# Two w_o groups of a decode kernel are loaded in two parts, one of them through a source with an outer dimension of 8

## The chip, the cores and the metric

The kernel runs on one core of a Trainium2 chip. The metric is the device time of one execution in microseconds (us); lower is better. A core has a matrix engine (PE, with its weight loads shown apart as PEld), a vector engine (DVE), a scalar engine (ACT), GpSimd (POOL), and SyncE (SP), which here does nothing but issue loads. Loads and stores are carried by 16 DMA engines that all issuers share.

## What is computed

One decode step: layer norm of a row x of 576 values, then two branches on it that are added to x. Branch A is attention with one query: 32 query heads, 16 key/value heads of 128, over the last 4096 positions of the caches, and a product with `wo`. Branch B is a gated MLP with sequence length 1. All tensors are bfloat16.

```python
xn = _layernorm(x, axis=-1)
# A
q = (xn @ wq).reshape(B, Sq, Hq, Dh).transpose(0, 2, 1, 3)
k = jnp.repeat(k_cache[:, :, Sk - W:, :], 2, axis=1)
v = jnp.repeat(v_cache[:, :, Sk - W:, :], 2, axis=1)
p = _softmax(jnp.einsum('bhqd,bhkd->bhqk', q, k) * Dh ** (-0.5), axis=-1)
o = jnp.einsum('bhqk,bhkd->bhqd', p, v)
a = o.transpose(0, 2, 1, 3).reshape(B, Sq, Hq * Dh) @ wo      # wo is 4096 x 576
# B
z = _gelu(xn @ w_in)                                          # w_in is 576 x 4608
g = w_sp * _layernorm(z[..., Fh:], axis=-1) + b_sp
b = (z[..., :Fh] * g) @ w_out                                 # w_out is 2304 x 576
out = x + a + b
```

Some 51 MB have to be read for a result of 576 values: 16 K and 16 V blocks of 1 MB, wq 4.7 MB, w_in 5.3 MB, wo 4.7 MB, w_out 2.7 MB.

## The kernel before, in words

**Loads.** All large loads are issued by SP, in program order, before any arithmetic of the program text: `load_kv` (line 81), `load_rows` (line 95, for wq, w_in and w_out) and `load_wo` (line 101). Their order is: K of heads 0 and 1, wq in five parts, and then for b = 1 to 8 the K of block b (two heads), the V of block b - 1, and a piece of w_in (b = 1 to 3) or one w_o group (`load_wo(b - 4)` for b = 4 to 6; in block 8 `load_wo(3)` stands in the place of K); at the end w_out in four parts of 8, 6, 3 and 1 rows a partition. Each load goes to a tile of the pool `units`, which has 18 buffers, and has one of eight completion semaphores in turn: a load is issued when the load eight before it, with the same semaphore, has landed. x and the two scalars of branch B come through ACT's queue (lines 70, 343, 344).

**A w_o group.** wo has 4096 rows; group j is rows 1024 j to 1024 j + 1023. `wo_v` gives partition p the eight consecutive rows 1024 j + 8 p + r, r = 0 to 7, as one run of 8 x 576 values, 9216 B. One load of 128 such runs fills the tile (line 101).

**Attention.** For each block b of two key/value heads, `T` (lines 203 to 207) transposes eight 128 x 128 pieces of K on PE and copies them out of PSUM on DVE or ACT, `S` (line 215) makes the scores, `sm_max`, `sm_tr`, `sm_exp` and `sm_rec` do the softmax, `PV` (line 258) multiplies with V, and `O` (line 263) writes four columns of `oTn`, 128 x 32, one column a query head: the head's 128 output values over the partitions.

**The product with wo.** In `oTn` the row 1024 j + i of wo belongs to partition i mod 128 of column 8 j + i div 128, while the tile has it at partition i div 8 and row r = i mod 8. `O_perm(j)` moves the values over: for each r a matmul (line 268) with `selr[:, r]`, which picks the partitions congruent to r modulo 8 and repeats them over the eight columns, gives all eight columns in every partition; line 271 multiplies with the mask `hm`, which keeps the one column that belongs to the partition (partitions 16 n to 16 n + 15 keep column n); line 273 adds up. The result, `oP[:, j, r]`, is the weight of the matmuls of `WO(j)` (line 277, through `out_mm`): 8 rows r in four column groups of 144, 32 matmuls a group. `selr` is made on DVE (line 189), `hm` too (line 133).

**Order.** The loop over b (lines 360 to 390) is the order of PE. `O_perm(j)` stands in blocks 2, 4, 6 and 8, `WO(j)` in blocks 4, 5, 6 and 8 (`wo_at`). The 18 rows of w_out follow as 72 matmuls of line 277, then line 395 copies the sum out of PSUM and line 396 stores it.

Of the kernel before, what the change touches and what calls it, by code (L numbers as in the profile page):

```python
# [8 lines left out]
FP32 = mybir.dt.float32  # L9
BF16 = mybir.dt.bfloat16  # L10
ALU = mybir.AluOpType
# [3 lines left out]
P = 128  # L15
D = 576
# [16 lines left out]
FR = FH // P  # L33
UNITS = 18
KTB = 12


@with_exitstack
def kernel(
# [14 lines left out]
    nc = tc.nc  # L54
    ctx.enter_context(tc.manual_schedule())

    const = ctx.enter_context(tc.tile_pool(name="const", bufs=1))
    work = ctx.enter_context(tc.tile_pool(name="work", bufs=2))
    units = ctx.enter_context(tc.tile_pool(name="units", bufs=UNITS))
    ktp = ctx.enter_context(tc.tile_pool(name="ktp", bufs=KTB))  # L60
    PS = bass.MemoryType.PSUM
# [11 lines left out]
    kn, vn, wq_t, win_t, wo_t, wout_t = {}, {}, {}, {}, {}, {}  # L73
    wq_v = A_wq.rearrange("k (s c) -> (k s) c", s=2).rearrange("(p r) c -> p r c", r=NS)
    win_v = B_w_in.rearrange("k (s c) -> (k s) c", s=2).rearrange("(p r) c -> p r c", r=NS)
    wo_v = A_wo.rearrange("(j p r) n -> j p (r n)", p=P, r=8)
    wout_v = B_w_out.rearrange("(p r) n -> p r n", r=FR)

    def load_kv(store, cache, name, h):
# [12 lines left out]
    def load_rows(store, view, name, width, cuts):  # L92
        for a, e in zip(cuts, cuts[1:]):
            t = units.tile([P, e - a, width], BF16, name=f"{name}{a}", tag="u")
            nc.sync.dma_start(t[:], view[:, a:e, :])
            for i in range(a, e):
                store[i] = t[:, i - a, :]

    def load_wo(j):
        t = units.tile([P, 8 * D], BF16, name=f"wo{j}", tag="u")  # L100
        nc.sync.dma_start(t[:], wo_v[j])
        wo_t[j] = t

    win_parts = {1: (0, 2, 4), 2: (4, 6, 8), 3: (8, 9)}
# [2 lines left out]
    for b in range(1, NB + 1):  # L107
        if b < NB:
            load_k(b)
        else:  # L110
            load_wo(NWO - 1)
        load_v(b - 1)
        if b in win_parts:
            load_rows(win_t, win_v, "win", FH, win_parts[b])
        elif b < 7:
            load_wo(b - 4)
# [3 lines left out]
    ident = const.tile([P, P], BF16, name="ident")  # L120
# [7 lines left out]
    ident_f = const.tile([P, P], FP32, name="ident_f")  # L128
# [3 lines left out]
    hm = const.tile([P, 8], FP32, name="hm")  # L132
    nc.vector.tensor_reduce(out=hm[:], in_=ident_f[:].rearrange("p (n q) -> p n q", n=8), axis=AXX, op=ALU.add)
    selr = const.tile([P, 8, 8, 16], BF16, name="selr")
    out_ps = ps_c.tile([P, OW], FP32, name="out_ps")
    nc.vector.memset(out_ps[:], 0.0)

# [49 lines left out]
        return xe_r[:, 2 * r:2 * r + 2]  # L187

    nc.vector.tensor_copy(selr[:], ident[:].rearrange("p (q r) -> p r q", r=8).unsqueeze(2).to_broadcast([P, 8, 8, 16]))


    kT, s_ps, p_sb, sm = {}, {}, {}, {}
    q_bf = const.tile([P, HQ], BF16, name="q_bf")
    oTn = const.tile([P, HQ], BF16, name="oTn")
    oP = const.tile([P, NWO, 8], BF16, name="oP")
# [68 lines left out]

    def O_perm(j):
        op = ps_m.tile([P, 8, 8], FP32, name=f"op{j}", tag="m")
        for r in range(8):
            nc.tensor.matmul(op[:, r, :], lhsT=selr[:, r, :, :].rearrange("p n q -> p (n q)"),  # L268
                             rhs=oTn[:, 8 * j:8 * j + 8], start=True, stop=True)
        tmp = work.tile([P, 8, 8], FP32, name=f"om{j}", tag="om")  # L270
        nc.vector.tensor_tensor(out=tmp[:], in0=op[:], in1=hm[:].unsqueeze(1).to_broadcast([P, 8, 8]), op=ALU.mult)
        with nc.allow_low_precision(reason="one of the eight is not zero, and it is a bfloat16 value"):
            nc.vector.tensor_reduce(out=oP[:, j, :], in_=tmp[:], axis=AXX, op=ALU.add)  # L273

    def out_mm(lhsT, rhs, start=False, last=False):
        for g in range(NCG):
            nc.tensor.matmul(out_ps[32 * g:32 * g + 1, :], lhsT=lhsT, rhs=rhs[:, OW * g:OW * (g + 1)],  # L277
                             start=start, stop=last, tile_position=(0, 32 * g))

    def WO(j):  # L280
        for r in range(8):
            out_mm(oP[:, j, r:r + 1], wo_t[j][:, D * r:D * (r + 1)])


    hv = const.tile([P, FR], BF16, name="hv")
# [50 lines left out]
    for r in range(NS):  # L336
        for c in range(16):
            nc.tensor.matmul(q_ps[:, c, :], lhsT=wq_t[r][:, P * c:P * (c + 1)], rhs=xe_of(r),  # L338
                             start=(r == 0 and c == 0), stop=r == NS - 1, skip_group_check=True)
# [5 lines left out]
    for g in range(NCG):  # L345
        nc.tensor.matmul(out_ps[32 * g:32 * g + 1, :], lhsT=one_bf[:, 0:1], rhs=x_row[:, OW * g:OW * (g + 1)],
                         start=True, stop=False, tile_position=(0, 32 * g))
# [12 lines left out]
    for b in range(1, NB + 1):  # L360
# [26 lines left out]
        if b % 2 == 0:  # L387
            O_perm(b // 2 - 1)
        if b in wo_at:
            WO(wo_at[b])  # L390
# [36 lines left out]
```

## Time and profile before

| | |
|---|---|
| median of 3 runs | 132.22 us (132.12 to 132.78) |
| profiled execution, its own time | 131.92 us |
| its span, first to last instruction | 130.1 us |
| PE, PEld busy | 106.3 us (82%), 100.7 us (77%) |
| DVE, ACT busy | 51.9 us (40%), 29.2 us (22%) |
| mean granted PE clock | 0.712 |
| bytes read | 50.96 MB, 392 GB/s over the span |
| chain of waits: DMA, PE, DVE | 45%, 44%, 6% of the span |
| a w_o load | 1152 KB, 20.6 us from issue to landing |

The profile is of one execution. Busy time is the time in which an engine ran an instruction; a matmul's end is modelled. "DMA share" is the mean busy share of the 16 DMA engines. "Landing" of a load is the moment when its semaphore has its full count. The chain of waits follows the execution back from its last instruction, at each step to what released it. Besides the summed rows the trace has a record of each DMA packet (queue, start, duration, bytes, but not which of the 16 engines ran it) and of each increment of a semaphore by a DMA.

### The profile page before, as it was taken

The page shows a single profiled execution, that of the slowest core. Times are in us where ns is not written, and L with a number is a line of the kernel's source. Part 1 is how long each engine was busy: PE and PEld are TensorE (multiplying, and loading weights), DVE is VectorE, ACT ScalarE, POOL GpSimd, SP SyncE. Part 2 cuts the span into 40 slices and gives each one's busy share as a digit, 9 for nine tenths or more (in the row PEclk, how much of TensorE's full clock was granted, in tenths as well). Part 3 has the DMA queues.
Part 4 walks back from the last instruction along what each step waited for, and adds up shares of the span by engine and source line. Part 5 has one row for each costly group of instructions (what it writes and reads, how often), then busy time and mean ns, then how long its engine had stood idle before and what let it go on. Part 6 is the DMA issues. An engine that isn't in the chain of part 4 may idle for free.

```text
span 130.1 us, 4613 instructions
## 1 busy us (share of the span) xinstructions
PE 106.3 (82%) x2133; PEld 100.7 (77%) x2133; DVE 51.9 (40%) x157; ACT 29.2 (22%) x38; POOL 0.7 (1%) x6
## 2 busy tenths in 40 slices
PE   3589518699899998989978798799899949994790
PEld 3489418499898997989977797699779939993780
DVE  4486000355402552054436624455444552454200
ACT  3136000033200360013604060233214401340000
POOL 2000000000000000000000000000000000000000
PEclk9999655556855599555995555557977985699559
DMA  4999999999999999999999999999999999999940
GB/s 116 420 431 431 420 412 422 418 420 429 411 415 420 421 416 419 413 415 418 423 415 418 424 425 408 430 411 420 418 422 412 420 421 416 415 420 417 388 158 0
DMA packets 7232, 51.24 MB, mean 394 GB/s; under 512 B 813, under 2 KB 942, under 8 KB 1454
## 3 DMA queue, kind: packets, MB, share of 16 engines
q1 hardware_dynamic: 7208, 50.96, 94.7%
q8 instruction: 16, 0.26, 0.8%
q14 instruction: 2, 0.02, 0.0%
q10 hardware_dynamic: 6, 0.00, 0.0%
HBM read 50.96 MB, written 0.00 MB: 392 GB/s over the span
## 4 chain that ended last, share of the span: by engine, by line
DMA 45%; PE 44%; DVE 6%; issue 1%; ACT 1%; ACTq 0%; SPq 0%
DMA k<-in_A_k_cache_dram 19%; PE tp L203 18%; DMA wout<-in_B_w_out_dram 14%; DMA wq<-in_A_wq_dram 12%; PE zp L294 8%; PE s L215 6%; PE o L258 5%; PE bc L234 2%; PE out_ps L277 1%; DVE m L227 1%; PE su L249 1%; PE tr L225 1%; PE op L268 1%; DVE mb L236 1%; ACT p L241 0%
## 5 line engine op out<-in xcount | busy, mean ns | idle before, releaser
L203 PE MATMUL tp<-ident,k 128*128 128x128 bf16 x512 | 53.0, 275 | 1.3 <-DMA k<-in_A_k_cache_dram 0.8
L203 PEld LDWEIGHTS <-k 128*128 128x128 bf16 x512 | 43.9, 128 | 2.7 <-issue 1.6
L207 DVE COPY kT<-tp 128x1024 bf16<-128x1024 bf16 x40 | 27.5, 690 | 23.5 <-PE tp L203 23.5
L205 ACT COPY kT<-tp 128x1024 bf16<-128x1024 bf16 x24 | 24.3, 1011 | 34.4 <-PE tp L203 34.4
L215 PE MATMUL s<-q_bf,kT 128*128 128x2 bf16 x512 | 21.0, 166 | 1.5 <-DVE kT L207 1.4
L215 PEld LDWEIGHTS <-kT 128*128 128x128 bf16 x512 | 19.9, 103 | 1.9 <-DVE kT L207 1.6
L258 PE MATMUL o<-p,v 128*128 128x2 bf16 x512 | 15.3, 164 | 0.1
L258 PEld LDWEIGHTS <-v 128*128 128x128 bf16 x512 | 14.4, 98 | 0.2 <-issue 0.2
L241 ACT ACTIVATE p<-d 128x128 bf16<-128x128 f32 x8 | 2.5, 310 | 49.9 <-DVE d L239 49.9
L294 PEld LDWEIGHTS <-win 128*128 128x128 bf16 x162 | 10.5, 162 | 1.6 <-issue 1.6
L294 PE MATMUL zp<-xe,win 128*128 128x2 bf16 x162 | 10.4, 200 | 1.1 <-DVE m L227 1.1
L338 PE MATMUL q_ps<-xe,wq 128*128 128x2 bf16 x144 | 4.5, 165 | 4.6 <-DMA wq<-in_A_wq_dram 4.6
L338 PEld LDWEIGHTS <-wq 128*128 128x128 bf16 x144 | 4.1, 101 | 4.9 <-DMA wq<-in_A_wq_dram 4.8
L234 PEld LDWEIGHTS bc<-dg,ones_f 4*128 4x128 f32 x16 | 3.2, 244 | 5.5 <-DVE dg L229 4.3
L234 PE MATMUL bc<-dg,ones_f 4*128 4x4 f32 x16 | 3.9, 309 | 4.0 <-DVE dg L229 3.1
L277 PE MATMUL out_ps<-wo,oP 128*1 128x144 bf16 x128 | 4.3, 296 | 1.8 <-DVE oP L273 1.6
L249 PEld LDWEIGHTS su<-ss,ones_f 128*128 128x128 f32 x16 | 4.3, 328 | 1.5 <-DVE ss L244 1.5
L249 PE MATMUL su<-ss,ones_f 128*128 128x4 f32 x16 | 4.4, 343 | 1.3 <-DVE ss L244 1.3
L220 DVE TENSOR_REDUCE mx<-s 128x4 f32<-128x128 f32 x8 | 2.3, 292 | 6.8 <-PE s L215 6.8
L277 PEld LDWEIGHTS <-oP 128*1 128x1 bf16 x128 | 2.9, 106 | 2.2 <-DVE oP L273 1.8
L244 DVE TENSOR_REDUCE ss<-p 128x4 f32<-128x128 bf16 x8 | 2.3, 286 | 3.2 <-ACT p L241 3.2
L340 DVE CAST q_bf<-q_ps 128x32 bf16<-128x32 f32 x1 | 0.3, 301 | 8.2 <-PE q_ps L338 8.2
(78 smaller groups left out, 41.3 us busy)
## 6 DMA issues: line engine op xcount, KB each, us to landing
k<-in_A_k_cache_dram SPq DMA_DIRECT2D x16, 1024.0 KB, 19.4
v<-in_A_v_cache_dram SPq DMA_DIRECT2D x16, 1024.0 KB, 20.6
win<-in_B_w_in_dram SPq DMA_DIRECT2D x4, 1152.0 KB, 18.9
wo<-in_A_wo_dram SPq DMA_DIRECT2D x4, 1152.0 KB, 20.6
wq<-in_A_wq_dram SPq DMA_DIRECT2D x4, 1024.0 KB, 10.9
wout<-in_B_w_out_dram SPq DMA_DIRECT2D x1, 1152.0 KB, 20.4
wout<-in_B_w_out_dram SPq DMA_DIRECT2D x1, 864.0 KB, 19.6
win<-in_B_w_in_dram SPq DMA_DIRECT2D x1, 576.0 KB, 19.3
```

Source lines behind the costliest of these rows:

```text
L203: nc.tensor.transpose(tp[:, i, :], kn[h][:, 8 * c + i, :], ident[:])
L205: nc.scalar.copy(kT[n][:], tp[:])
L207: nc.vector.tensor_copy(kT[n][:], tp[:])
L215: nc.tensor.matmul(s_ps[b][:, i, 8 * c + t, :], lhsT=kT[n][:, t, :], rhs=q_bf[:, 2 * h:2 * h + 2], start=True, stop=True)
L220: nc.vector.tensor_reduce(out=mx[:], in_=s_ps[b][:].rearrange("p i t r -> p i r t"), axis=AXX, op=ALU.max)
L234: nc.tensor.matmul(bc[:], lhsT=ones_f[0:4, :], rhs=sm[b]["dg"][:], start=True, stop=True)
L241: nc.scalar.activation(p[:], d[:], ACT.Exp, scale=SCALE)
L249: nc.tensor.matmul(su[:], lhsT=ones_f[:], rhs=sm[b]["ss"][:].rearrange("p i r -> p (i r)"), start=True, stop=True)
L258: nc.tensor.matmul(sm[b]["o"][:, 2 * i:2 * i + 2], lhsT=vn[2 * b + i][:, t, :], rhs=p_sb[b][:, i, t, :], start=t == 0, stop=t == NT - 1)
L277: nc.tensor.matmul(out_ps[32 * g:32 * g + 1, :], lhsT=lhsT, rhs=rhs[:, OW * g:OW * (g + 1)], start=start, stop=last, tile_position=(0, 32 ...
L294: nc.tensor.matmul(zp[:, c, :], lhsT=w_r[:, c, :], rhs=xe_of(r), start=(r == rows.start and c == 0), stop=r == rows.stop - 1, skip_group_c ...
L338: nc.tensor.matmul(q_ps[:, c, :], lhsT=wq_t[r][:, P * c:P * (c + 1)], rhs=xe_of(r), start=(r == 0 and c == 0), stop=r == NS - 1, skip_grou ...
```

## The change

Groups 0 and 3 are each loaded by two loads in place of one. The first brings rows r = 0 to n - 1 of each partition (n = 3 for group 0, 2 for group 3), 128 runs of n x 1152 B. Its source is written with the group's 1024 rows split as (q, a, r) = (16, 8, 8) and `a` taken outermost, so it has the dimensions 8 x 16 x (n x 576), and partition 16 a + q gets rows 64 q + 8 a + r, where before partition p had rows 8 p + r. The second load brings the rows from n on as before, 128 runs of (8 - n) x 1152 B. Groups 1 and 2 keep one load.

As these n rows stand at other partitions, `O_perm` needs another selection (`selw`) and another mask (`hmw`) for them; the multiplication with the mask is done in two pieces in groups 0 and 3. `hmw` is one more reduction on DVE at the start and `selw` three more copies of 128 columns, after `selr`. The matmuls keep their number and shapes.

```diff
+WIDE = {0: 3, 3: 2}
+NWIDE = 3
...
-    wo_v = A_wo.rearrange("(j p r) n -> j p (r n)", p=P, r=8)
+    wo_v = A_wo.rearrange("(j p r) n -> j p r n", p=P, r=8)
...
     def load_wo(j):
-        t = units.tile([P, 8 * D], BF16, name=f"wo{j}", tag="u")
-        nc.sync.dma_start(t[:], wo_v[j])
+        t = units.tile([P, 8, D], BF16, name=f"wo{j}", tag="u")
+        n = WIDE.get(j, 0)
+        if n:
+            nc.sync.dma_start(t[:, 0:n, :].rearrange("p r n -> p (r n)"),
+                              A_wo[1024 * j:1024 * (j + 1), :].rearrange("(q a r) n -> a q (r n)", a=8, r=8)[:, :, 0:n * D])
+        nc.sync.dma_start(t[:, n:8, :], wo_v[j][:, n:8, :])
         wo_t[j] = t
...
+    hmw = const.tile([P, 8], FP32, name="hmw")
+    nc.vector.tensor_reduce(out=hmw[:], in_=ident_f[:].rearrange("p (a n q) -> p n a q", a=8, n=8),
+                            axis=mybir.AxisListType.XY, op=ALU.add)
+    selw = const.tile([P, NWIDE, P], BF16, name="selw")
...
+    for r in range(NWIDE):
+        nc.vector.tensor_copy(selw[:, r, :].rearrange("p (a n q) -> p a n q", a=8, n=8),
+                              ident[:].rearrange("p (q a r) -> p r a q", q=2, a=8)[:, r].unsqueeze(2).to_broadcast([P, 8, 8, 2]))
...
     def O_perm(j):
         op = ps_m.tile([P, 8, 8], FP32, name=f"op{j}", tag="m")
+        n = WIDE.get(j, 0)
         for r in range(8):
-            nc.tensor.matmul(op[:, r, :], lhsT=selr[:, r, :, :].rearrange("p n q -> p (n q)"),
-                             rhs=oTn[:, 8 * j:8 * j + 8], start=True, stop=True)
+            sel = selw[:, r, :] if r < n else selr[:, r, :, :].rearrange("p n q -> p (n q)")
+            nc.tensor.matmul(op[:, r, :], lhsT=sel, rhs=oTn[:, 8 * j:8 * j + 8], start=True, stop=True)
         tmp = work.tile([P, 8, 8], FP32, name=f"om{j}", tag="om")
-        nc.vector.tensor_tensor(out=tmp[:], in0=op[:], in1=hm[:].unsqueeze(1).to_broadcast([P, 8, 8]), op=ALU.mult)
+        for a, e, mask in ((0, n, hmw), (n, 8, hm)):
+            if e > a:
+                nc.vector.tensor_tensor(out=tmp[:, a:e, :], in0=op[:, a:e, :],
+                                        in1=mask[:].unsqueeze(1).to_broadcast([P, e - a, 8]), op=ALU.mult)
...
     def WO(j):
         for r in range(8):
-            out_mm(oP[:, j, r:r + 1], wo_t[j][:, D * r:D * (r + 1)])
+            out_mm(oP[:, j, r:r + 1], wo_t[j][:, r, :])
```

## The prediction

> **What bounds the kernel now.** I read the DMA rows of the page first, then the last microseconds as a table of stretches, then the waits and the tail of the timeline, and last the trace's own records of DMA packets and semaphore landings.
>
> ```profile
> DMA  4999999999999999999999999999999999999940
> GB/s 116 420 431 431 420 412 422 418 420 429 411 415 420 421 416 419 413 415 418 423 415 418 424 425 408 430 411 420 418 422 412 420 421 416 415 420 417 388 158 0
> ...
> q1 hardware_dynamic: 7208, 50.96, 94.7%
> q8 instruction: 16, 0.26, 0.8%
> q14 instruction: 2, 0.02, 0.0%
> ```
>
> All 16 DMA engines are busy from slice 2 to slice 38. The q8 row is instructions, not data: 16 packets of 16 KB; 0.8% of 16 engines x 130.1 us is 16.7 us, so 1.04 us each, on one engine. The next rows (stretch, length, busy PE, PEld, DVE, ACT, POOL, then PE clock, DMA share, GB/s) show that the 16 engines do not finish together:
>
> ```profile
> 122.00:123.00 1.00, 0.60 (x18) 0.45 (x14) 0.28 (x2) 0.00 (x0) 0.00 (x0) 0.50 1.00 407
> 123.00:123.50 0.50, 0.08 (x7) 0.08 (x9) 0.33 (x2) 0.00 (x0) 0.00 (x0) 0.50 0.82 327
> 123.50:124.00 0.50, 0.50 (x24) 0.50 (x26) 0.00 (x0) 0.00 (x0) 0.00 (x0) 0.50 0.63 253
> 124.00:125.00 1.00, 1.00 (x44) 1.00 (x36) 0.00 (x0) 0.00 (x0) 0.00 (x0) 0.50 0.53 204
> 125.00:126.00 1.00, 1.00 (x40) 0.80 (x32) 0.00 (x0) 0.00 (x0) 0.00 (x0) 0.50 0.43 174
> 126.00:126.50 0.50, 0.38 (x16) 0.18 (x5) 0.00 (x0) 0.00 (x0) 0.00 (x0) 0.50 0.26 92
> ```
>
> About half of them are done by 124, the rest at 126.4. Shares times lengths from 123 on add up to 1.82 us, so perfectly shared work would end at 124.8: at most 1.6 us lie in balance. The landings say who is late. Every 128-row load raises its semaphore 16 times, once an engine; for the last wout part these come 0.00 to 0.32 us (six engines), 0.96 and 1.01, 1.71, and 3.10 to 3.34 us (seven) after the first, at 123.52. The same lags can be followed back load by load: each 16 KB packet of q8 puts one engine back by 1.55 us, always one of the same eight in turn; each 8 KB packet of q14 puts one of two others back by about 0.7.
>
> But PE ends at almost the same time:
>
> ```profile
> 122.89 0.23 DVE L271 TENSOR_TENSOR om<-op,hm 128x64 f32<-128x64 f32 x1 [0.44 <-PE op L268]
> 123.14 0.22 DVE L273 TENSOR_REDUCE oP<-om 128x8 bf16<-128x64 f32 x1
> ...
> 123.42 1.13 PE L277 MATMUL out_ps<-wo,oP 128*1 128x144 bf16 x32 [0.57 <-DVE oP L273]
> ...
> 124.33 2.05 PE L277 MATMUL out_ps<-wout,hv 128*1 128x144 bf16 x56
> ...
> 126.55 0.59 PE L277 MATMUL out_ps<-wout,hv 128*1 128x144 bf16 x16 [0.17 <-DMA wout<-in_B_w_out_dram]
> ```
>
> In the list of waits PE's only wait on a load after the first 21 us is this one:
>
> ```profile
> PE out_ps L277 <- DMA wout<-in_B_w_out_dram: 0.2, 1, 0.2
> ```
>
> PE ends its 56 matmuls at 126.38 and needs 0.59 for the last 16. Earlier loads alone can save 0.17 us; later loads cost nearly all that they are late.
>
> **The change, step by step.** *Who carries the moved rows.* The landings also show how a load is spread: one row (x_row) raises its semaphore once from a transfer, the output's four rows four times, 128 rows 16 times. A load with an outer dimension of 8 on one side should thus run on eight engines. [...]
>
> *Engine time.* From one packet's start to the next on its engine the records have 47 ns for 1152 B, 132 for 3456, 176 for 4608, 262 for 6912, 309 for 8192, 346 for 9216; between neighbours, 2304 B is 90 and 5760 B 219 (estimates). A w_o load is now 8 x 346 + 6 (semaphore) = 2774 ns on each engine. With three rows moved, all engines do 8 x 219 + 6 = 1758, and the eight carriers 16 x 132 + 6 = 2118 more: 3876, so +1102 for carriers and -1016 for the others. With two rows: 8 x 262 + 6 = 2102, carriers 16 x 90 + 6 more = 3548: +774 and -672. Together carriers +1.88, others -1.69 us.
>
> *Are the carriers the early ones?* The two 2-byte loads of lines 343 and 344 run on one engine, which is a carrier too if a load on fewer engines always takes the first ones. Their packets, at 15.13 and 16.06, push back the packets of one engine alone by 6 ns each. Following it, it becomes one of a pair that I can't part at 23.5; one of the pair takes the instruction packet of 24.5. The small loads' semaphores come 463 and 464 ns after their packet; the engine hit at 24.5 shows 448 on average, the other of the pair about 462. So I take the carriers for the early engines, at 4 to 1.
>
> *Full speed or not.* Eight carriers reach all 128 partitions, of which 16 engines have eight each in a plain load, so half of the wide packets or more go where another engine writes, beside its normal stream. No row shows two engines on each other's partitions. Lower bound: full speed, 0 extra. Upper bound: two engines share and each has half, so the wide 16 x 132 + 16 x 90 = 3.55 us take 3.55 more. Nearest row: the instruction packet, the only big one that does not go to its engine's own rows: 1.04 us where 16 KB at 309 ns per 8 KB would take 0.62, a factor of 1.7. I take 1.75, that is 0.75 x 3.55 = 2.66 us extra.
>
> [...]
>
> *Sum for the loads.* Carriers: 0.32 (the last without an instruction packet) + 1.88 + 2.66 = 4.86 us behind the first engine of now; those two with an 8 KB packet 1.01 + 1.88 + 2.66 = 5.55. Now the last is at 3.34. A landing waits for all engines, so the end moves by 5.55 - 3.34 = +2.2.
>
> *The rest.* Two more load issues on SP at 0.33 us: SP stands waiting for a landing eight loads back nearly all the time, and with some 20 us from issue to landing, two half loads among eight leave over 15 us of queued data; uncovered they would cost 0.66. That the second part waits for the first, both being of one tile, is unlikely: the two loads into ws2 were issued at 11.68 and 11.93, the first landed at 15.90. hmw: one reduce as hm's (0.28), in DVE's 0.86 us idle before line 147. Three selw copies: selr took 1.08 for 1024 columns, 128 each are some 0.2 (line 140's copy of 128): 0.6 us ahead of the first kT copy, covered by 8.2 us in which DVE waits for q_ps; uncovered 0.9 in all. O_perm of groups 0 and 3 has one more small multiply, about 0.2 us. For group 3 it lies between 122.89 and 123.42 on the way to WO(3), so PE's own tail would end 0.2 later, 0.03 after today's end; beside loads 2.2 late it is hidden. Matmuls and weight loads keep number and shape.
>
> Profiled execution 131.92 + 2.1 (PE was 0.1 us behind the last part) = 134.0; the median, 132.22, lies 0.30 above that execution: **134.3 us**, slower by 1.6%.
>
> **Rivals.** *Balance works, PE ends it.* Carriers early and at full speed: the ends are 0.32 + 1.88 = 2.20 and, with an 8 KB packet, 2.89 for carriers, 3.34 - 1.69 = 1.65 for the others: loads end 0.45 earlier, but PE's tail plus 0.2 gives +0.03: 132.25. For it: the moved time, 3.57 us between halves, fits the gap of 3.3. Against: full speed on foreign partitions is unproven. Chance 0.17. *Balance works and PE follows.* k and v land 1.0 us earlier from group 0 on; if PE or its clock (0.50 at the end) gained from it, the gain is 0.45 to 1.1 (the two 8 KB packets on other engines): 131.4. Against: PE's one 0.17 us wait. Chance 0.13. *Carriers are the late ones, or mixed.* Full speed: 3.34 + 1.88, the end +1.9: 134.1. Decided by the identity above. Chance 0.15. *The load does not narrow* and runs on 16: two semaphores and some more packets, 0.1 us: 132.3. Chance 0.05. *Forecast*, slowed carriers, 0.50; by its bounds from 132.2 (no extra) over 135.2 (half) up to some 137, where three writers meet (a third of the speed: 3.55 x 2 instead of 2.66, +4.4).
>
> **From these.** Its own range is 132.9 to 136.8; with the rivals 131.8 to 136.8. 0.5%, 0.66 us, is about what a measurement can tell from no change. Faster: 0.12. Within: 0.17 + 0.05 + 0.04 (low end of the forecast and of the gain) = 0.26. Slower: 0.62.
>
> **What would show it.** Landings of the two wide loads raised by eight engines; their packets of 3456 and 2304 B at more than 132 and 90 ns; the DMA share below 1 after about 124 for longer, with the end at 128 or later and PE waiting at line 277 for a wout part by 2 us. I am wrong if the wide packets keep 132 and 90 ns (then one of the full-speed rivals holds, and the order of the last landings says which), if 16 engines carry them, or if PE waits for k or v.

## The result and the profile after

| | before | after |
|---|---|---|
| median | 132.12 us (132.09 to 132.78, 6 runs) | 137.67 us (137.49 to 138.00, 6 runs) |
| ratio, 95% interval | | 1.0415 (1.0391 to 1.0438) |
| profiled execution; its span | 131.92; 130.1 us | 137.75; 136.0 us |
| last w_out load: landings of its 16 engines | 123.52 to 126.86 us | 125.92 to 132.76 us |

The change costs 5.55 us, 4.2%. The direction was foretold, the time lies 3.4 us above the forecast and 0.9 us outside the range. The page of the kernel after, its rows for DMA:

```profile
DMA  4999999999999999999999999999999999999710
GB/s 121 424 427 429 422 412 424 417 426 419 421 412 423 422 418 417 417 420 414 422 409 251 306 417 425 415 419 419 424 416 423 412 422 306 313 415 410 317 50 0
...
q1 hardware_dynamic: 7480, 50.96, 93.8%
q8 instruction: 16, 0.26, 0.8%
```

The bytes are those of before, and the engines are as busy as before, but in slices 21 and 22, and again in 33 and 34 (counted from 0, 3.4 us each), they move 251 to 313 GB/s where the neighbours have about 418. Against 418 GB/s these four slices lack (167 + 112 + 112 + 105) / 418 x 3.4 = 4.03 us of full transfer. They are the times at which groups 0 and 3 are loaded. Packets take longer there; what holds them up, this view does not say.

The second trace of the loss is in the last microseconds. Rows of the table of stretches (stretch, length, busy PE, PEld, DVE, ACT, POOL, PE clock, DMA share, GB/s):

```profile
123.00:124.00 1.00, 0.00 (x0) 0.00 (x0) 0.00 (x0) 0.00 (x0) 0.00 (x0) 0.50 0.94 394
...
126.00:127.00 1.00, 0.49 (x18) 0.49 (x19) 0.00 (x0) 0.00 (x0) 0.00 (x0) 0.50 0.83 344
...
128.00:129.00 1.00, 0.37 (x17) 0.28 (x18) 0.51 (x3) 0.00 (x0) 0.00 (x0) 0.50 0.69 270
129.00:130.00 1.00, 1.00 (x44) 1.00 (x36) 0.00 (x0) 0.00 (x0) 0.00 (x0) 0.50 0.24 96
...
131.00:132.00 1.00, 0.62 (x24) 0.62 (x24) 0.00 (x0) 0.00 (x0) 0.00 (x0) 0.50 0.10 40
132.00:133.00 1.00, 0.81 (x28) 0.46 (x16) 0.00 (x0) 0.00 (x0) 0.00 (x0) 0.50 0.02 6
```

A DMA share of 0.10 is less than two engines of 16. From 130 on, nearly everything waits for two engines that are late. Before, the last 3 us were carried by about seven engines.

PE's waits and the tail of the timeline (start, duration, and in brackets the idle time before and what ended it; lines 273 and 296 here are 258 and 277 of before):

```profile
PE o L273 <- DMA v<-in_A_v_cache_dram: 4.0, 2, 2.5
...
PE out_ps L296 <- DMA wout<-in_B_w_out_dram: 0.7, 2, 0.5
```

```profile
128.77 1.13 PE L296 MATMUL out_ps<-wo,oP 128*1 128x144 bf16 x32 [0.63 <-DVE oP L292]
...
129.68 1.18 PE L296 MATMUL out_ps<-wout,hv 128*1 128x144 bf16 x32
...
131.38 0.89 PE L296 MATMUL out_ps<-wout,hv 128*1 128x144 bf16 x24 [0.52 <-DMA wout<-in_B_w_out_dram]
...
132.45 0.65 PE L296 MATMUL out_ps<-wout,hv 128*1 128x144 bf16 x16 [0.19 <-DMA wout<-in_B_w_out_dram]
```

PE now waits 4.0 us for V blocks, which it did not before, and the last matmuls follow the last w_out part again. The waits for V are idle time ahead of a PE that catches up before the end; what ends the kernel is the late engines.

**Following the engines.** The records of packets don't name their engine, but nearly every packet starts within 10 ns of the end of another (99.8% of those from 25 to 118 us before, 97.9% after), so the start of a packet can be matched with the end of the one before on its engine. Eight engines show 16 packets of 3456 B in a row (the carriers), eight none. Ends of the last data packets in the kernel after (an own evaluation of the records; a landing is seen 0.43 to 0.47 us later):

```
no carrier, no 16 KB instruction packet:      125.49 125.74
no carrier, instruction packets:              126.89 128.49 128.54 128.60 128.65 128.68
carrier, no instruction packet:               128.88 128.98 129.17 129.22
carrier, an 8 KB packet of q14:               129.77 130.04
carrier, instruction packets:                 131.66 132.29
```

Six of the eight engines that take the 16 KB packets are not carriers, two are, and these two end last. Each of the two w_o loads through the changed source raises its semaphore once about 1 us after its issue (at 57.93 us for group 0) and then eight times from a transfer (74.65 to 77.67 us), so it does run on eight engines. No row of before could show it: the counts there were 1, 4 and 16.

### The profile page after: what moved, and what is told of

It reads as the page before. It is cut to its first block, busy times and chain, and to the rows that moved or that the text cites. A ratio compares the mean times of both kernels' runs of the same rounds, so it can differ in the third digit from the quotient of the medians.

```text
span 136.0 us, 4622 instructions
## 1 busy us (share of the span) xinstructions
PE 108.0 (79%) x2133; PEld 102.3 (75%) x2133; DVE 52.6 (39%) x163; ACT 29.2 (21%) x38; POOL 0.7 (1%) x6
## 4 chain that ended last, share of the span: by engine, by line
PE 59%; DMA 28%; DVE 8%; issue 2%; ACT 1%; ACTq 0%
PE tp L218 26%; DMA wout<-in_B_w_out_dram 13%; DMA wq<-in_A_wq_dram 11%; PE s L230 8%; PE zp L313 8%; PE o L273 7%; DMA k<-in_A_k_cache_dram 3%; PE out_ps L296 3%; PE bc L249 3%; PE su L264 1%; DVE m L242 1%; PE tr L240 1%; ACT p L256 1%; DVE dg L244 1%; DVE d L254 1%
## 5 line engine op out<-in xcount | busy, mean ns | idle before, releaser
L218 PE MATMUL tp<-ident,k 128*128 128x128 bf16 x512 | 53.7, 278 | 1.6 <-DVE kT L222 0.9
L218 PEld LDWEIGHTS <-k 128*128 128x128 bf16 x512 | 44.8, 130 | 3.0 <-issue 2.2
L278 DVE TENSOR_TENSOR oTn<-o,rm 128x4 bf16<-128x4 f32 x8 | 1.3, 162 | 10.0 <-PE o L273 10.0
```

The costliest lines, as they stand in the source:

```text
L218: nc.tensor.transpose(tp[:, i, :], kn[h][:, 8 * c + i, :], ident[:])
```

## The experiments

The theory after the result: an engine loses time while it writes partitions that another engine is writing, and so does the other one. The rivals: the two-part loads cost by themselves; eight engines in place of 16 cost by themselves; reading rows that lie far apart in memory costs; the late end alone explains it.

**s1: only the split.** Three and two rows in a load of their own, but from the plain source, 128 runs in the old order.

The kernel before with this edit:

```diff
-        nc.sync.dma_start(t[:], wo_v[j])
+        n = {0: 3, 3: 2}.get(j, 0)
+        if n:
+            nc.sync.dma_start(t[:, 0:n * D], wo_v[j][:, 0:n * D])
+        nc.sync.dma_start(t[:, n * D:8 * D], wo_v[j][:, n * D:8 * D])
```

> The kernel before with groups 0 and 3 loaded in two parts of 3 + 5 and 2 + 6 rows, both parts with the 128 partitions outermost and the rows at their old places. All theories: 16 landings for each part, 132.2 to 132.4 us (two more load issues and some shorter packets). If the time is near 137, it is the splitting, and not the eight engines or the other order, that costs.

132.12 us, ratio 0.9997 (0.9985 to 1.0009). The split, with its issues and semaphores, costs nothing that these runs can tell (under 0.2%).

**a1: group 0 alone.**

```diff
-WIDE = {0: 3, 3: 2}
+WIDE = {0: 3}
```

> The changed kernel with group 0 alone in the new way, group 3 as before. Sharing theory (engines that write each other's partitions slow one another while the wide part runs): a cost by the moved rows, 3 of 5, so 132.1 + 3/5 x 5.5 = 135.4 us, and the dip of the DMA rate around 70 us alone. If only what happens late counts (an early delay lies under PE's slack): under 133.5.

135.26 us, ratio 1.0236 (1.0220 to 1.0251). GB/s falls in slices 21 to 23 only (300, 260, 382). 3.1 of 5.55 us for 3 of 5 rows: the cost goes with the moved rows.

**x0 to x5: extra loads.** To vary source and target freely, these leave the kernel as it was before and add loads of the same 3 and 2 rows a partition, 0.74 MB in all, into a buffer that nothing reads. Of the lines marked x0 to x5 each run has only its own.

```diff
     def load_wo(j):
+        n = {0: 3, 3: 2}.get(j, 0)
+        if n:
+            x = units.tile([P, 8 * D], BF16, name=f"xt{j}", tag="u")
+            by8 = A_wo[1024 * j:1024 * (j + 1), :].rearrange("(q a r) n -> a q (r n)", a=8, r=8)
+            nc.sync.dma_start(x[:, 0:n * D], wo_v[j][:, 0:n * D])                      # x0
+            nc.sync.dma_start(x[:, 0:n * D], by8[:, :, 0:n * D])                       # x1
+            for h in range(2):                                                         # x2; x3: partitions 64 + 32 * h
+                nc.sync.dma_start(x[32 * h:32 * h + 32, 0:2 * n * D], by8[:, 4 * h:4 * h + 4, 0:2 * n * D])
+            nc.sync.dma_start(x[0:64, 0:2 * n * D], by8[:, 0:8, 0:2 * n * D])          # x4
+            # x5: 16 on the outside, "(q a r) n -> a q (r n)", a=16, r=4, to all 128 partitions
```

x0, plain:

> The kernel before with extra loads of wo rows into a tile that nothing reads, ahead of groups 0 and 3: 3 and 2 rows a partition, 128 partitions outermost. The price of the bytes alone: 8 x 135 ns and 8 x 93 ns on each engine, +1.8 us less the 0.1 to 0.2 that PE was waiting: 133.7 to 134.0 us, packets of plain loads at their old 312 ns (8192 B). Same by all theories.

x1, through the change's source and order:

> As the extra loads before, but through the change's source: outer dimension 8, partition 16 a + q. The w_o loads themselves are untouched. Sharing theory: the wide packets take 1.4 to 1.7 times their plain 135 and 93 ns, plain packets beside them 350 ns and more, time some 138.5 to 139.5 us. Rival (an eight-engine load costs only its own engine time, and it is the late engines that carry it): plain packets stay at 312, carriers +2.1 and +1.5 us, 135.6 us.

x2, through a source of outer dimension 8 as well, but to partitions 0 to 63 in loads of 32, so that block a of the source goes to four partitions from 4a and four from 32 + 4a (that one engine brings one block is my reading, here and in x3 to c3; no record shows which partitions an engine writes):

> Extra loads of the same bytes through sources of outer dimension 8, but to partitions 0 to 63 only, in two loads of 32 partitions each (engine a gets 32 h + 4 a to 32 h + 4 a + 3), runs of 6912 and 4608 B. [...] Rivals (eight engines are slow in themselves, or the reads 64 rows apart are): as the extra loads in the change's way, 138.5 or more.

x3, the same to partitions 64 to 127:

> The same loads to partitions 64 to 127. Sharing theory: each carrier now writes where exactly one engine outside the eight writes its plain stream; both slow: packets of 6912 B at 350 to 520 ns, plain packets beside them slow on the eight others alone, 137 to 139 us. Rivals that look at the reads or at the number of engines only: the same time as for partitions 0 to 63.

x4, partitions 0 to 63 in one load, block a at 8a to 8a + 7:

> The same bytes to partitions 0 to 63 in one load of 64 partitions, so that engine a writes partitions 8 a to 8 a + 7. [...]

x5, all 16 engines, block a at 8a to 8a + 7:

> The same bytes through a source with outer dimension 16, partition 8 a + q: all 16 engines carry, but in the other order of blocks. [...] If the cost is that of eight engines only: 133.8 as with the plain extra load.

Packets are the mean of the extra load for group 0, then of the plain w_o load of 9216 B behind it; "lacking" is the sum over the slices under 390 GB/s (the first and the last three left out), worked out as above.

| | median us | ratio (95%) | extra, 9216 B packet, ns | lacking us |
|---|---|---|---|---|
| x0 plain | 133.81 | 1.0126 (1.0109 to 1.0142) | 3456 B: 136; 350 | 0 |
| x1 as the change | 139.79 | 1.0579 (1.0564 to 1.0595) | 3456 B: 213; 514 | 4.3 |
| x2 0 to 63, by 32 | 135.40 | 1.0230 (1.0195 to 1.0264) | 6912 B: 266; 351 | 0 |
| x3 64 to 127, by 32 | 142.17 | 1.0728 (1.0685 to 1.0770) | 6912 B: 487; 590 | 6.8 |
| x4 0 to 63, one load | 140.33 | 1.0502 (1.0402 to 1.0603) | 6912 B: 396; 441 | 2.9 |
| x5 16 engines | 137.02 | 1.0349 (1.0309 to 1.0389) | 3456 B: 206; 450 | 3.3 |

x2 and x3 read the same rows through sources of the same form and differ only in the partitions written: 6.8 us apart, as much as x3 lacks. The page of x2, then of x3:

```profile
GB/s 120 426 426 429 414 422 421 414 423 421 415 417 419 433 406 428 404 416 417 426 414 423 424 405 427 420 418 417 418 421 417 415 421 415 419 419 405 300 49 0
```

```profile
GB/s 136 422 424 431 407 426 424 415 426 413 421 415 427 422 413 413 414 418 417 417 282 215 343 426 417 417 421 422 414 419 424 415 362 230 263 412 413 337 61 0
```

x2 had been expected at 135.5 us, with 8 x 262 and 8 x 176 ns more on the carriers and no packet slowed; it took 135.40. No dip in x2: neither eight engines nor reads far apart are slow here (packets of 6912 B take 266 ns, as those of the w_out part before). What x2 pays over x0, 1.6 us, is the carriers' longer work, seen as landings of the last load spread over 6.8 us. x4 says that it isn't the upper half as such, and x5 that it isn't the narrowing: with all 16 engines at work and landings spread over 3.3 us as before, another order of partitions alone cost 3.2 us more than x0. That was more than I had expected.

x4's four runs lie far apart: its median is of all four (138.05 to 140.8), its ratio of the two lowest, 138.05 and 140.04, and its profile of the lowest, so its size is not to be relied on. Three expectations were too low: x1, expected at 138.5 to 139.5, took 139.79, x3, at 137 to 139, took 142.17, and x5, at 134.5 to 136, took 137.02. For x4, 136.5 to 139 us had been expected, an estimate from an assumption on which engines meet that no run shows. For x3 only the packets of the eight other engines were expected to be slow, and for x4 only those of the carriers; the records say otherwise, below ("Who loses").

**c1: the change, by 32 partitions.** The moved part comes in four loads of 32 partitions each, and the moved rows are used, as in the change, with selection and mask to match.

```diff
-            nc.sync.dma_start(t[:, 0:n, :].rearrange("p r n -> p (r n)"),
-                              A_wo[1024 * j:1024 * (j + 1), :].rearrange("(q a r) n -> a q (r n)", a=8, r=8)[:, :, 0:n * D])
+            by8 = A_wo[1024 * j:1024 * (j + 1), :].rearrange("(q a r) n -> a q (r n)", a=8, r=8)
+            for h in range(4):
+                nc.sync.dma_start(t[32 * h:32 * h + 32, 0:n, :].rearrange("p r n -> p (r n)"), by8[:, 4 * h:4 * h + 4, 0:n * D])
...
```

> [...] Theory (the loss is engines writing on partitions that another engine is writing): packets of 3456, 2304, 5760 and 8192 B keep their durations of before, no dip in GB/s, and what stays is the carriers' own time, 1.88 us on the two late engines that are carriers: 132.1 + 1.9 = 134.0 us, 133.4 to 134.7. Rival (the loss comes with eight engines or with the order in which memory is read, whatever the partitions): 136.5 to 138, as the change. Second rival (the eight loads with their semaphores cost by themselves): over 134.7 with packets at plain durations.

137.75 us, ratio 1.0424 (1.0406 to 1.0441): as slow as the change, the expectation missed by 3.7 us. It took for granted that by 32 partitions every engine writes only what it writes in a plain load. That could not be so: a plain load has 128 packets and 16 landings, eight packets an engine, so the eight carriers write 64 partitions in it, not 128, and x3's packets to partitions 64 to 127 had been slow (487 ns for 6912 B). The records say so packet by packet. Durations of the packets of 3456 B in the order of their start, 16 at a time; each load has 32 of them, so the first 64, nearly in this order, go to partitions 0 to 63, the others to 64 to 127:

```
start from, us   70.74  71.22  71.66  72.03  72.42  72.92  73.53  74.65
mean, ns           135    135    135    172    264    274    225    228
```

The packet takes 135 ns as long as the moved rows go to partitions 0 to 63, and up to 264 to 274 ns, twice that, once they go to 64 to 127. c1's table of stretches in the same time:

```profile
70.00:71.00 1.00, 1.00 (x11) 1.00 (x10) 0.63 (x4) 0.61 (x2) 0.00 (x0) 0.50 0.97 402
71.00:72.00 1.00, 0.36 (x4) 0.09 (x1) 0.93 (x6) 0.53 (x1) 0.00 (x0) 0.50 0.99 405
72.00:73.00 1.00, 0.53 (x12) 0.54 (x13) 1.00 (x3) 0.00 (x0) 0.00 (x0) 0.50 1.09 272
73.00:74.00 1.00, 1.00 (x18) 1.00 (x17) 0.32 (x2) 0.00 (x0) 0.00 (x0) 0.50 1.08 222
74.00:75.00 1.00, 1.00 (x18) 1.00 (x16) 0.45 (x1) 0.18 (x1) 0.00 (x0) 0.50 1.01 298
```

The rate holds (402 and 405 GB/s) while the first two of the four loads run and falls to about half (222 GB/s) when the third begins; the DMA share stays at 0.97 to 1.09.

**c2 and c3: the change, with the moved rows in one half.** The same bytes, engines and second loads as the change, but the moved rows go to a buffer of their own, 2n rows on each of 64 partitions. These two time the loads and do not compute the kernel's result: the moved rows meet weights of other rows, in 2n x 4 matmuls over 64 partitions in place of n x 4 over 128.

```diff
+            x = wide_t[j] = units.tile([P, 8, D], BF16, name=f"xw{j}", tag="u")
+            for h in range(2):                                                         # c3: partitions 64 + 32 * h
+                nc.sync.dma_start(x[32 * h:32 * h + 32, 0:2 * n, :].rearrange("p r n -> p (r n)"),
+                                  by8[:, 4 * h:4 * h + 4, 0:2 * n * D])
...
     def WO(j):
+        for r in range(2 * n):
+            out_mm(oP[0:64, j, r:r + 1], wide_t[j][0:64, r, :])                        # c3: 64:128
+        for r in range(n, 8):
```

> The change with the same moved bytes, on the same eight engines and beside the same second loads, brought to partitions 0 to 63 alone, 2n rows each, in two loads of 32 partitions into a buffer of their own; the product takes them in 2n times 4 matmuls of 64 rows. Changed in the computation: the moved rows are multiplied with weights of other rows. Theory (c1 put only half of the moved bytes on partitions of their own engines: the eight carriers write 0 to 63 in plain loads, the other eight engines 64 to 127): all packets at plain durations, no dip in GB/s, and what stays is the carriers' own 1.88 us on the two late engines that are carriers: 132.1 + 1.9 = 134.0, 133.3 to 134.8. Rival (eight engines or the small loads cost by themselves): as c1 and the change, 136.5 to 138.

> As c2, but to partitions 64 to 127. Same change in the computation: the moved rows are multiplied with weights of other rows. Theory (all moved bytes now go where the other eight engines write): wide packets of 6912 and 4608 B at about twice 266 and 180 ns, the others beside them also longer, GB/s down to 200 to 280 twice; by the difference of x3 and x2, 6.8 us, 134.0 + 6.8 = 140.8, 139 to 142. Rival (it is eight engines as such): the same time as c2.

c2: 133.74 us, ratio 1.0110 (1.0080 to 1.0140). c3: 140.32 us, ratio 1.0593 (1.0560 to 1.0626). Both within what was expected, 6.6 us apart for the choice of 64 partitions. In c2 the packets have their plain durations in the mean (6912 B 265 ns, 5760 B 227, 4608 B 180, 8192 B 315 beside them), in c3 they take 490, 398, 323 and 382. The page of c2, then c3's table of stretches:

```profile
GB/s 95 428 428 425 430 412 419 415 428 424 412 418 415 427 422 414 418 420 418 415 425 407 419 417 420 421 417 425 421 422 410 421 416 416 418 421 406 316 56 0
```

```profile
72.00:74.00 2.00, 1.87 (x30) 1.87 (x31) 1.32 (x4) 0.00 (x0) 0.00 (x0) 0.50 1.00 208
74.00:76.00 2.00, 2.00 (x34) 2.00 (x32) 0.56 (x2) 1.01 (x1) 0.00 (x0) 0.50 1.05 229
76.00:78.00 2.00, 2.00 (x53) 2.00 (x51) 0.82 (x2) 1.01 (x1) 0.00 (x0) 0.76 0.95 207
```

For 6 us the engines move 207 to 229 GB/s, half of 418. The theory of c2 and c3, that in plain loads the carriers write partitions 0 to 63 and the other eight engines 64 to 127, fits x2, x3, c1, c2 and c3; the partitions of an engine stand in no record, and what limits the rate in c3 is not shown.

**Who loses.** If only the two engines that meet shared their time, each would lose what the wide packets take at full speed: in x3 8 x 262 + 8 x 176 ns = 3.5 us. x3 lacks 6.8. The records of packets under way at one moment show that more is slow than those two (duration in ns; plain: 8192 B 312, 9216 B 349, 6912 B 264, 5760 B 225, 3456 B 135):

```
                  moved rows under way     all other packets under way
x3, at 77.00 us   2 of 6912 B: 519, 520    14: 8192 B 587 to 593, 9216 B 661 to 700
x4, at 72.00 us   5 of 6912 B: 542 to 554  11: 8192 B 627 to 645, 9216 B 704 to 722
after, at 75.75   2 of 3456 B: 218, 218    14: 5760 B 365 to 385, 8192 B 506 to 518
x2, at 72.00 us   6 of 6912 B: 265 to 271  10: 8192 B 312 to 315, 9216 B 349, 349
```

All 16 packets under way are slow together and by nearly the same factor (1.9 to 2.0 in x3, 2.0 to 2.1 in x4, 1.6 to 1.7 in the kernel after), although in x3 only two carriers still bring moved rows then, and in x4 all moved rows go to partitions 0 to 63, where those of x2 slowed nothing. c3 moves 207 GB/s from 76 to 78 us with three carriers or fewer still at it. So where the moved rows go decides whether there is a loss (x2 against x3, 6.8 us; c2 against c3, 6.6), and the loss is not confined to the engines that bring them. That it starts where engines meet on partitions is my explanation; neither this nor how the loss reaches the other engines is shown by a run here.

**The sum.** What c2 costs, 133.74 - 132.29 = 1.45 us, is the carriers' longer work at full speed. What GB/s lacks in the kernel after, 4.03 us, is the slow stretches. Together 5.5, and 5.55 were measured. By the same sum x1 is 133.81 + 1.6 + 4.3 = 139.7 (139.79), x3 142.2 (142.17), x5, without carriers, 137.1 (137.02), and c1, with the 1.45 of c2 and 3.75 lacking, 137.3 (137.75); x4 comes to 138.3, where its profiled run took 138.05. c3 comes to 139.4 where 140.32 was measured; its profiled run, from which the 5.7 us lacking are taken, took 139.71, so 0.3 to 0.9 us stay open. None of the variants is faster than before: the best that a narrow load gives here is c2's, to partitions 0 to 63, 1.1% slower than before.

## Why the prediction was partly right

Two steps failed: the identity of the carriers, and the size and the place of the slowing.

**The bound and the tail** hold: the loads end the kernel, one wait for a w_out part precedes PE's last 16 matmuls, and everything else that the change adds (issues on SP, `hmw`, `selw`, the divided multiplication, the second load) is hidden, as s1 and c2 show together.

**Eight carriers, and their engine time** hold. Without slow stretches, in c2, the first landing of the last w_out load comes 1.59 us earlier than before (121.93) and the last 1.59 later (128.45); -1.69 and +1.88 were worked out.

**"Are the carriers the early ones?"** failed; this is the larger part of the miss. Taken for early at 4 to 1, they are in truth mixed: six of eight are early, but the two that also take 16 KB packets set the end. The landings of c2 say so without following any engine: two engines at 121.93 and 122.21 us, twelve from 123.62 to 126.25, two at 128.44 and 128.45, so two of the early engines were made earlier and two of the late ones later. The forecast let the end start from a lag of 1.01 us (an early carrier with an 8 KB packet), and it starts from 3.34: 2.33 us. The working inferred one engine from pushes of 6 ns, on the condition that a load on fewer engines always takes the same first ones, which no row of before shows, and then spoke for all eight; two groups of eight need not be equal or opposite. The rival "Carriers are the late ones, or mixed", full speed, 134.1, is near what c2 measured: 133.74. It left out only the slow stretches, which c2 does not have.

**"Full speed or not"** named a condition that fits the runs, moved rows that go where another engine writes (c3 against c2: 6.6 us), but the size and the place were off: 2.66 us were charged to the carriers' own wide packets, and nothing to the plain loads. The wide packets take 214 ns (136 in s1) for 3456 B and 132 (93 at full speed) for 2304 B, factors of 1.6 and 1.4 where 1.75 was taken after the instruction packet (1.04 us for 16 KB), which no run shows to be slow for this reason: 16 x 78 + 16 x 39 ns = 1.9 us on a carrier. The larger part is lost in plain packets, on all 16 engines: those of 5760 B take 348 ns (225 in s1), K and V packets between 70 and 81 us take 358 (315 before). Engine by engine: a non-carrier without instruction packets lands its last part at 125.92, 2.4 us after its time before, where 1.69 less was due: 4.1 us lost. The latest carrier lands at 132.76, 5.9 us after 126.86, of which 1.88 is its work: 4.0 lost. Carriers and others alike lose about 4.0 us, where 2.66 on the carriers alone was forecast: 1.3 us more.

2.33 + 1.3 = 3.6 us by which the loads end later than forecast (5.9 in place of 2.2, with rounding); the time was missed by 3.4. The upper end, "some 137, where three writers meet", came near the time for another reason: the longest of the wide packets of group 0 took 251 ns, less than twice 135, and not three times; three writers at one place are shown by no run. Nor does it follow from its own sum: +4.4 on the forecast of 134.3 is 138.7.

**The rivals** with a gain needed full speed and early carriers; neither held. "The load does not narrow" is excluded by the eight landings. "PE waits for k or v" was named as a sign of being wrong: PE does wait 4.0 us for V (not at all before, 1.3 us in c2, 6.1 in c3); the end is still set by w_out.

## What to carry to other kernels

In a kernel bound by loads, look at which partitions a load fills and in which order, not only at how many engines it uses: in some orders the extra packets and the plain ones beside them were slow here, also when all 16 engines carried the load (x5: 206 ns for 3456 B, 450 for 9216 B, where x0 has 136 and 350). Slices in which DMA is fully busy but GB/s is low show this at a glance, and (usual rate - rate) / usual rate x their length came to its price within 0.5 us in the runs of the sum above, c3 apart. Before an imbalance of engines is used, the late engines have to be identified one by one: here the loads on eight of them lengthened two of the late ones too, and in c2 the last landing came 1.59 us later for it.

## What was not expected of the hardware

- When moved rows go to partitions 64 to 127 beside the plain loads, the packets of all 16 engines are slow: in c1 135 becomes 264 to 274 ns (3456 B) and 93 becomes 186 (2304 B), and in c3 the total falls to half (207 to 229 GB/s of 418), also while three carriers or fewer still bring moved rows.
- The instruction packets of 16 KB go through eight engines, two of which belong to the eight that the narrow loads use here. Each puts its engine back by 1.55 us, and nothing in this kernel evens the engines out before its end: two such packets are the 3.1 us and more by which the late engines land after the first.
- Moving 0.74 MB in another order of partitions cost 3.2 us (x5 over x0), twice what its transfer cost at all (x0 over before: 1.7 us).
